# First batch of a gated linear attention: float32 operands on TensorE, keys transposed by TensorE, tap diagonals written by ScalarE

## The chip, the cores and the metric

The kernel runs on one core of one Trainium2 chip. The metric is the device time of one execution in microseconds (us). Engines are named as the profile names them: PE is TensorE (PEld its weight loads), DVE is VectorE, ACT is ScalarE, POOL is GpSimd, SP is SyncE, which here only issues transfers. f16 and f32 are float16 and float32.

## What is computed

Four batches go through three stages. The first is a linear attention with a forget gate per channel; the second a causal convolution of 5 taps that gates a projection; the third a two-dimensional Fourier mix, a normalisation and a two-layer perceptron.

```python
# attention: 4 batches, 8 heads, 768 tokens, 48 channels a head
f = 1.0 / (1.0 + np.exp(-f_logit))
for t in range(S):
    state = f[:, :, t, :, None] * state + np.einsum('bhd,bhe->bhde', k[:, :, t], v[:, :, t])
    y[:, :, t] = np.einsum('bhd,bhde->bhe', q[:, :, t], state)
# gating: 384 channels
gate = sigmoid(causal_conv(x, conv_w))            # 5 taps
x = gate * (x @ w_val) @ w_out
# mix and perceptron
u = x + np.real(fft2(x))
ch = np.maximum(normalised(u) @ w_ch1, 0.0) @ w_ch2
out = u + ch
```

## The kernel before

Everything is float32 at its ends and f16 on TensorE: an operand is split into a high f16 part (written by ACT) and a low f16 part (DVE or POOL subtracts the high one), and a product is three f16 products, high by high, high by low and low by high, added up in PSUM.

A batch of 768 tokens is 6 chunks of 128 (`NC`), and two chunks share one preparation. `Prep` loads the forget logits `f` and the tile `qk` (queries and keys, channels of two heads on 128 partitions, 4 head pairs), forms running sums of log gates on DVE (the scan `f<-sep,f`), their exponentials `e` and `f` on ACT, and multiplies them into `qk` in four steps (`scaled`), each on DVE or POOL by a string of letters: `E0` for the first preparation, `E1` for the others. `Attention.split` makes the f16 parts of a chunk: `qkhl` (ACT high, DVE low), `vz` from the values `v` (ACT high, DVE low), and sends the keys through a transposing DMA into `kt`. `Attention.scores` forms keys by queries, 24 matmuls a chunk into two PSUM tiles; DVE multiplies them by the causal mask into `a`, ACT writes the high part `ah`, POOL the low part `al` of the first half and DVE that of the second (`LO`). `Attention.outputs` forms the chunk's contribution to the state (12 matmuls with `kt`, not in the last chunk), the output `y` (24 matmuls with `vz`), the part from the state so far (12 matmuls with `tb`, not in the first chunk), then updates the state `T` on DVE and splits it into `tb` (ACT high, DVE low). The output goes to `xT` on ACT, partly on through a DMA, and is split again into `xhl`.

In the first batch the convolution is done partly by TensorE: `diagonals` writes 15 taps in two f16 parts as 30 diagonal matrices of 128 by 128 into `fs`, by two POOL instructions, and four of the six gate units multiply `xhl` by them. The tile `fs` is later overwritten by the tables of the Fourier mix. Between the steps of the first batch's attention, other generators are advanced: `small_weights` (`w_out`, `w_val` and the tables made of them) and `mlp_weights`, which decodes the perceptron's weights `w` from 64-bit storage by three DVE steps, a scaling and a high part on ACT and a low part on POOL. 30 matmuls on the constant tile `sep` (`keep_warm(c, PRE)`) stand ahead of the first batch and two more behind each of its first steps; nothing reads their result.

The order of instructions on each engine is set when the program is built, by a scheduler that works from priorities; an instruction's priority is its place in the code, except where `at(c, n)` gives it the fixed place `n`: `LATER` for the perceptron's weights and the second batch's preparations. On the chip each engine runs its list in order.

```python
e.tensor_tensor(parts[:, 1], qk, parts[:, 0], ALU.subtract)          # split: qkhl, low part
nc.sync.dma_start_transpose(out=kt, in_=hl[:, 1].rearrange("p l a w -> p (l a w)"))
for n, (lk, lq) in enumerate(((0, 0), (0, 1), (1, 0))):              # scores: three f16 products
```

Of the kernel before, what the change touches and what calls it, by code (L numbers as in the profile page):

```python
# [22 lines left out]
KT = DM // 128  # L23
# [119 lines left out]
def load_constants(c):  # L143
    nc, T, io = c.nc, c.T, c.io
    c.ident = T([128, 128], F32, "ident")
    nc.sync.dma_start(c.ident, io["ident"])
    c.mask = T([128, CH], F32, "mask")
    nc.sync.dma_start(c.mask, io["mask"])
    c.small = T([128, 5], F32, "small")
    nc.sync.dma_start(c.small, io["small"])  # L150
    c.bmask, c.vs, c.pad, c.bias = c.small[:, 0:2], c.small[:, 2:3], c.small[:, 3:4], c.small[:, 4:5]
    c.ends = T([128, NB, 2, NC, NP], F32, "ends")
    c.pm = T([128, NB, NC, NP, 2], F32, "pm")
    c.xmax = T([128, NB], F32, "xmax")
# [72 lines left out]
def diagonals(c):  # L227
# [9 lines left out]
    nc.gpsimd.tensor_tensor(w[:, 1], w[:, 1], w[:, 0], ALU.subtract)  # L237
    for l in range(2):
        nc.gpsimd.tensor_tensor(c.diagonal[:, l].rearrange("p k t m -> p (k t) m"), c.ident.unsqueeze(1).to_broadcast([128, n, 128]),
                                w[:, l].unsqueeze(2).to_broadcast([128, n, 128]), ALU.mult)  # L240


def small_weights(c):
# [227 lines left out]
class Attention:  # L471
# [19 lines left out]
    def split(self, g):  # L491

        c, nc = self.c, self.c.nc
        b, i = g // NC, g % NC
        qk = self.preps[g // TC].qk[:, :, :, g % TC].rearrange("p a x h w -> p a x (h w)")
        hl = c.T([128, 2, 2, NP, CH], F16, "hl", 2, name="qkhl")
# [7 lines left out]
        self.kt[g] = kt  # L504
        v = self.v.pop(g).rearrange("p (h e) -> p h e", h=NH)
        if i == 0:
            nc.vector.tensor_reduce(c.seen[:, b, 1], v, AX.X, ALU.max, apply_absolute_value=True)
        vz = c.vz[g % 2][:, 0:2 * NH * 2 * HD].rearrange("p (l h w) -> p l h w", l=2, h=NH)[:, :, :, 0:HD]
        nc.scalar.activation(vz[:, 0], v, AF.Copy, scale=c.vs)
        nc.vector.scalar_tensor_tensor(vz[:, 1], v, c.vs, vz[:, 0], ALU.mult, ALU.subtract)  # L510

    def scores(self, g):

        c, nc, hl = self.c, self.c.nc, self.hl[g]
        ps = [c.PS(NP * CH, "p", 4) for _ in range(2)]
# [14 lines left out]
    def outputs(self, g, x):  # L530

        c, nc, mm = self.c, self.c.nc, self.c.mm
        b, i = g // NC, g % NC
        w = 2 * HD
        hl, kt = self.hl.pop(g), self.kt.pop(g).rearrange("p (l a) w -> p l a w", l=2)
# [26 lines left out]
        if i < NC - 1:  # L562
            state = c.state
            pm = c.pm[:, b, i].unsqueeze(3).to_broadcast([128, NP, 2, HD])
            new = ds
            if i:
                nc.vector.tensor_tensor(state, new, state, ALU.add)
                new = state
            nc.vector.tensor_tensor(state, new, pm, ALU.mult)
            parts = c.tb[(i + 1) % 2][:, 0:2 * NP * w].rearrange("p (l w) -> p l w", l=2)  # L570
            flat = state.rearrange("p a h e -> p (a h e)")
# [3 lines left out]
        y4 = y[0:w].rearrange("p (a w) -> p a w", a=NP)  # L575
        at = TAPS - 1 + i * CH
        xf = x.f[0:w, :, at:at + CH]
        nc.scalar.activation(xf[:, :, SUB:], y4[:, :, SUB:], AF.Copy, scale=X_SCALE / OUT_FAR)
        nc.scalar.activation(xf[:, :, SUB - 1::-1], y4[:, :, 0:SUB], AF.Copy, scale=X_SCALE / OUT_NEAR)
        for k in range(KT):  # L580
            nc.sync.dma_start(x.f[w:, k, at:at + CH], x.f[32 * k:32 * k + 32, KT, at:at + CH])
        yield

# [339 lines left out]
def emit(tc, io):  # L923
    c = setup(tc, io)
    with tc.tile_pool(name="sb", bufs=1) as pool, tc.tile_pool(name="ps", bufs=1, space=bass.MemoryType.PSUM) as psum:
# [24 lines left out]
        def others(g):  # L950

            u = g // 2 + 2
            if u < NB * NT:
                if g % 2 == 0:
                    steps[u] = att.preps[u].steps(E1)
                    for _ in range(2):
# [3 lines left out]

        first, second = small, mlp_weights(c, (W1_SCALE, W2_SCALE))
        c.pieces = 0
# [17 lines left out]
        def abc():  # L980
            for b in range(NB):
# [4 lines left out]
                for n, v in enumerate(att.batch(b, x, todo, others)):  # L986
                    if b == 0:
                        aside(first, SIDE[n] if n < len(SIDE) else 1)
                        if n >= WFROM:
                            aside(second, 1, LATER)  # L990
# [19 lines left out]
DEC = 'vvvvvvvvvvvv'  # L1010
E0 = 'vgvg'
E1 = 'gggv'
LO = 'vgv'
# [11 lines left out]
WFROM = 8  # L1025
LATER = 1150
MULTIPLIED = ((0, 0), (0, 1), (0, 2), (1, 0))
# [358 lines left out]
```

## Time and profile before

| | us |
|---|---|
| median of 3 runs | 654.32 |
| lowest and highest run | 653.95, 656.33 |
| the profiled execution | 652.6 |
| its span, first to last instruction | 650.8 |
| mean granted TensorE clock | 0.939 of full speed |

| engine | busy us | share of the span |
|---|---|---|
| PE | 574.1 | 88% |
| DVE | 463.2 | 71% |
| ACT | 292.6 | 45% |
| POOL | 240.6 | 37% |

The shares are means over stages with different limits. The page's row of 40 slices shows this: in the first eight slices (130 us) DVE is at 7 to 9 tenths and PE mostly at 3 to 8, behind them PE is at 9 or more in nearly all. A reading by stage is therefore needed, and the rows for it stand in the section below. Matmul durations in the rows contain the pipeline's depth; what a matmul takes from the engine is the distance between two starts.

### The profile page before, as it was taken

Reading aid. Unit: us, or ns where it says so; the run is one execution under the profiler, and the core shown is the slowest. Engines: PE = TensorE matmul, PEld = TensorE weight load, DVE = VectorE, ACT = ScalarE, POOL = GpSimd, SP = SyncE. Lnnn points to the kernel's source line nnn. Section 1 sums busy time; section 2 is a strip of 40 time slices with the busy share of each in tenths; the row PEclk is TensorE's granted clock in tenths of the full one; section 3 lists DMA queues with packets and bytes.
Section 4 is the critical chain, followed back from the end, with each engine's and each line's share of the span. In section 5 each row is a group of like instructions: output and inputs, shape, how many; then the busy total and the mean of one; then the engine's idle time right before and its main releaser. Section 6 shows DMA issues by size and latency. Waiting matters only on the chain.

```text
span 650.8 us, 12244 instructions
## 1 busy us (share of the span) xinstructions
PE 574.1 (88%) x4920; PEld 409.3 (63%) x4920; DVE 463.2 (71%) x729; ACT 292.6 (45%) x508; POOL 240.6 (37%) x248
## 2 busy tenths in 40 slices
PE   5357865869996899999998999999999999999995
PEld 2135453447675666776677776775677777777773
DVE  5899999787979889346579789265397492463651
ACT  3467687453576664221376644212465532121110
POOL 3778657342457451112348333021362221130000
PEclk9558878789999999999988999999999999999998
DMA  8616775921425560002225440011212000041000
GB/s 310 188 57 202 173 174 148 264 83 49 91 65 168 146 155 32 26 14 61 41 60 175 113 113 25 1 46 29 44 45 66 7 25 1 20 63 41 1 26 30
DMA packets 64435, 54.99 MB, mean 84 GB/s; under 512 B 46416, under 2 KB 55888, under 8 KB 64368
## 3 DMA queue, kind: packets, MB, share of 16 engines
q1 hardware_dynamic: 63824, 52.27, 30.3%
q0 software_dynamic: 544, 1.84, 0.9%
q8 instruction: 40, 0.66, 0.4%
q14 instruction: 27, 0.22, 0.1%
HBM read 37.58 MB, written 4.72 MB: 65 GB/s over the span
## 4 chain that ended last, share of the span: by engine, by line
PE 45%; DVE 26%; DMA 11%; issue 6%; ACT 5%; POOL 4%; SPq 2%; DVEq 0%; POOLq 0%; ACTq 0%
PE c L80 28%; PE p L80 17%; DVE gate L80 6%; DMA qk<-in_qk 4%; DVE w L80 3%; DMA w<-in_w_ch 3%; DVE qkhl L80 2%; SPq L80 2%; DVE eo L80 2%; DMA xT<-xT 2%; DMA f<-in_f 1%; DVE f L80 1%; POOL gd L80 1%; DVE vz L80 1%; DVE hl L80 1%
## 5 line engine op out<-in xcount | busy, mean ns | idle before, releaser
L80 PE MATMUL c<-unT,w 128*128 128x256 f16 x1296 | 193.5, 274 | 0.6 <-DVE unT L80 0.6
L80 PE MATMUL c<-w,hh 128*128 128x384 f16 x576 | 149.7, 327 | 3.3 <-ACT w L80 1.9
L80 PEld LDWEIGHTS <-w 128*128 128x128 f16 x1296 | 126.5, 98 | 23.7 <-issue 0.7
L80 PE MATMUL c<-w,hl 128*128 128x384 f16 x288 | 92.6, 327 | 0.5 <-DVE hl L80 0.5
L80 DVE SCALAR_TENSOR_TENSOR hl<-c,hh 128x512 f16<-128x512 f32 x72 | 49.3, 685 | 60.4 <-ACT hh L80 60.2
L80 ACT ACTIVATE hh<-c 128x512 f16<-128x512 f32 x72 | 42.4, 589 | 94.5 <-PE c L80 92.4
L80 PEld LDWEIGHTS <-hh 128*128 128x128 f16 x576 | 56.1, 98 | 32.9 <-issue 3.7
L80 PE MATMUL p<-qkhl 64*128 64x128 f16 x576 | 54.0, 234 | 22.7 <-DVE qkhl L80 15.3
L80 PEld LDWEIGHTS <-gd 128*128 128x128 f16 x468 | 44.5, 99 | 27.1 <-issue 6.9
L80 PEld LDWEIGHTS <-qkhl 64*128 64x128 f16 x576 | 28.9, 100 | 48.1 <-issue 26.5
L80 PE MATMUL p<-wp,gd 128*128 128x388 f16 x216 | 55.0, 341 | 3.2 <-DVE xc L80 3.2
L80 PE MATMUL p<-ah,vz 128*128 128x128 f16 x384 | 56.2, 233 | 0.0
L80 PEld LDWEIGHTS <-vz 128*128 128x128 f16 x576 | 47.8, 105 | 9.6 <-issue 4.8
L80 POOL TENSOR_TENSOR al<-a,ah 128x512 f16<-128x512 f32 x24 | 37.6, 1566 | 31.0 <-ACT ah L80 31.0
L80 POOL TENSOR_TENSOR xhl<-xT,xhl 128x384 f16<-128x384 f32 x23 | 26.9, 1170 | 54.0 <-ACT xhl L80 54.0
L80 DVE SCALAR_TENSOR_TENSOR gate<-xT,convw,gate 128x768 f32<-128x768 f32 (+1 forms) x44 | 41.5, 996 | 7.1 <-ACT gate L80 7.0
L80 POOL TENSOR_TENSOR rs<-rs,mhalf 128x2 f32<-128x2 f32 x12 | 9.4, 780 | 99.9 <-DVE rs L80 99.9
L80 DVE TENSOR_TENSOR a<-p,mask 128x512 f32<-128x512 f32 x48 | 30.9, 680 | 21.0 <-PE p L80 18.0
L80 PE MATMUL p<-wch,gd 128*128 128x194 f16 x252 | 41.2, 247 | 5.2 <-DVE gd L80 1.8
L80 PE MATMUL p<-al,vz 128*128 128x128 f16 x192 | 41.5, 233 | 3.6 <-DVE al L80 2.4
L80 PE MATMUL p<-xhl,wv 128*128 128x384 f16 x216 | 43.1, 328 | 1.3 <-DVE a L80 0.6
L80 POOL TENSOR_TENSOR qk<-qk,e 128x512 f32<-128x512 f32 x23 | 31.7, 1396 | 32.4 <-ACT e L80 10.1
(149 smaller groups left out, 1068.9 us busy)
## 6 DMA issues: line engine op xcount, KB each, us to landing
qk<-in_qk SPq DMA_DIRECT2D x24, 512.0 KB, 5.4
w<-in_w_ch SPq DMA_DIRECT2D x21, 384.0 KB, 4.4
f<-in_f SPq DMA_DIRECT2D x12, 528.0 KB, 4.2
v<-in_v SPq DMA_DIRECT2D x24, 192.0 KB, 2.8
out_dram<-ot SPq DMA_DIRECT2D x24, 192.0 KB, 1.9
raw<-in_w_out SPq DMA_DIRECT2D x3, 384.0 KB, 4.5
vraw<-in_w_val SPq DMA_DIRECT2D x3, 384.0 KB, 8.0
xT<-xT SPq DMA_DIRECT2D x72, 16.0 KB, 1.8
```

The lines of the kernel that those rows point to most:

```text
L80: r = f(*args, **kw)
```

## The change

For the first batch (`g < NC`) the attention works on float32 operands instead of f16 parts. `whole` takes the place of `split`: four TensorE transposes bring the keys into PSUM, ACT copies them to `ktf`, and ACT scales the values into `vz`, seen as float32. `whole_scores` has 8 float32 matmuls where there were 24 f16 ones, and DVE's masked product `af` is used as it is, without `ah` and `al`. `whole_outputs` has 4, 8 and 4 float32 matmuls where there were 12, 24 and 12; the state is copied to `tb` by one ACT instruction. The other batches go through the code of before (`split_outputs`), and before they use the two `vz` tiles POOL clears them again. `diagonals` becomes a generator: 30 ACT instructions, two to a step, take the place of the two on POOL. The first preparation's four products all go to DVE (`E0`), of the second and third two each (`E1`, one before); the later ones stay as they were (`E2`). `LATER` is 880 where it was 1150.

```diff
-    for l in range(2):
-        nc.gpsimd.tensor_tensor(c.diagonal[:, l].rearrange("p k t m -> p (k t) m"), c.ident.unsqueeze(1).to_broadcast([128, n, 128]),
-                                w[:, l].unsqueeze(2).to_broadcast([128, n, 128]), ALU.mult)
+    for i in range(n):
+        for l in range(2):
+            nc.scalar.activation(c.diagonal[:, l, i // TAPS, i % TAPS], c.ident, AF.Copy, scale=w[:, l, i:i + 1])
+        if i % 2:
+            yield
+    yield
...
+        if b == 0:
+            return self.whole(g, v)
+        if i < 2:
+            nc.gpsimd.memset(c.vz[i].bitcast(U32), 0)
...
+    def whole(self, g, v):
+        c, nc = self.c, self.c.nc
+        qk = self.preps[g // TC].qk[:, :, :, g % TC].rearrange("p a x h w -> p a x (h w)")
+        ps = c.PS(NP * CH, "c1", 2)
+        for p in range(NP):
+            c.tr(ps[:, p * CH:(p + 1) * CH], qk[:, p, 1], c.ident)
+        kt = c.T([128, NP, 128], F32, "kt", 2, name="ktf")
+        nc.scalar.activation(kt.rearrange("p a w -> p (a w)"), ps, AF.Copy)
+        nc.scalar.activation(c.vz[g % 2].bitcast(F32).rearrange("p (h w) -> p h w", h=NH)[:, :, 0:HD], v, AF.Copy, scale=c.vs)
+        self.hl[g], self.kt[g] = qk, kt
+
+    def whole_scores(self, g):
...
+            for p in range(NP):
+                r = slice(64 * hh, 64 * hh + 64)
+                c.mm(ps[:, p * CH:(p + 1) * CH], qk[r, p, 1], qk[r, p, 0], p == 0, p == NP - 1)
+            a = c.T([128, NP, CH], F32, tag, 2, name="af")
+            nc.vector.tensor_tensor(a, ps.rearrange("p (a w) -> p a w", a=NP), c.mask.unsqueeze(1).to_broadcast([128, NP, CH]), ALU.mult)
+            self.a[g].append(a)
+
+    def whole_outputs(self, g):
...
+            for p in range(NP):
+                mm(ds[:, p], kt[:, p], vc[:, p], p == 0, p == NP - 1)
...
+        for p in range(NP):
+            for hh in range(2):
+                mm(y[:, p * CH:(p + 1) * CH], vz[:, (2 * p + hh) * w - HD * hh:][:, 0:128], a[hh][:, p], p == hh == 0,
+                   i == 0 and hh == 1 and p == NP - 1)
...
+                mm(y[:, p * CH:(p + 1) * CH], c.tb[i % 2].bitcast(F32)[:, p * w:][:, 0:128], qk[:, p, 0], False, p == NP - 1)
+        if i < NC - 1:
+            self.new_state(g, ds)
+            nc.scalar.activation(c.tb[(i + 1) % 2].bitcast(F32)[:, 0:NP * w], c.state.rearrange("p a h e -> p (a h e)"), AF.Copy,
+                                 scale=A_SCALE)
...
-E0 = 'vgvg'
-E1 = 'gggv'
+E0 = 'vvvv'
+E1, E2 = 'vgvg', 'gggv'
...
-LATER = 1150
+LATER = 880
```

PE's list at the start of the first batch, before (`sep` is the constant tile of the 30 matmuls ahead, `qkhl` the f16 parts of queries and keys, `raw` a piece of `w_out`):

```order
L80 LDWEIGHTS sep_61
L80 MATMUL c1_186<-sep_61 128x512
L80 LDWEIGHTS qkhl_148
L80 MATMUL p_288<-qkhl_148 128x128
L80 LDWEIGHTS qkhl_148
L80 MATMUL p_289<-qkhl_148 128x128
```

The same place on PE now, with the transposed keys in `c_140` and `c_150`:

```order
L80 MATMUL c_140<-ident,qk 128x128 x4
L80 MATMUL c_150<-ident,qk 128x128 x4
L80 MATMUL p<-qk 128x128 x16
L80 LDWEIGHTS sep
L80 MATMUL c_179<-sep 128x512
```

The 30 matmuls on `sep` stood ahead of all work; now they stand behind the transposes and scores of the first two chunks, and ahead of the first chunk's outputs.

DVE's list behind the first scaling of `qk`, before:

```order
L80 TENSOR_TENSOR qk<-qk,f 128x4x2x64
L80 SCALAR_TENSOR_TENSOR raw<-raw,bits 128x384
L80 TENSOR_SCALAR bits<-raw 128x384
L80 SCALAR_TENSOR_TENSOR bits<-raw,bits 128x384
L80 TENSOR_TENSOR qkhl<-qk,qkhl 128x4x2x128
L80 SCALAR_TENSOR_TENSOR raw<-raw,bits 128x384
L80 TENSOR_TENSOR qkhl<-qk,qkhl 128x4x2x128
L80 TENSOR_TENSOR wpm<-raw 128x192 x2
```

And now, where `af` is the masked scores:

```order
L80 TENSOR_TENSOR qk<-qk,e 128x4x2x64
L80 TENSOR_SCALAR bits<-raw 128x384
L80 TENSOR_TENSOR qk<-qk,f 128x4x2x64 x2
L80 SCALAR_TENSOR_TENSOR bits<-raw,bits 128x384
L80 SCALAR_TENSOR_TENSOR raw<-raw,bits 128x384
L80 TENSOR_SCALAR bits<-raw 128x384
L80 SCALAR_TENSOR_TENSOR bits<-raw,bits 128x384
L80 SCALAR_TENSOR_TENSOR raw<-raw,bits 128x384
L80 TENSOR_SCALAR bits<-raw 128x384
L80 SCALAR_TENSOR_TENSOR bits<-raw,bits 128x384
L80 TENSOR_TENSOR af<-p,mask 128x512
```

Two `qkhl` are gone, two products of `qk` came from POOL, and the first `af` has moved ahead of the third piece's last step.

ACT's list at the same time, before:

```order
L80 ACTIVATE f<-f 128x1056
L80 ACTIVATE qkhl<-qk 128x4x2x128 x2
L80 ACTIVATE raw<-raw 128x384 x2
L80 ACTIVATE vz_91<-v,small 128x8x48
L80 ACTIVATE f<-f 128x1056
L80 ACTIVATE ah<-a 128x512
```

And now, with the diagonals in `fs`:

```order
L80 ACTIVATE f<-f 128x1056
L80 ACTIVATE fs<-ident,cwf 128x128 x20
L80 ACTIVATE ktf<-c_140 128x512
L80 ACTIVATE raw<-raw 128x384
L80 ACTIVATE fs<-ident,cwf 128x128
L80 ACTIVATE ktf<-c_150 128x512
```

Twenty of the 30 diagonals stand ahead of the first copy of transposed keys, on which PE's first matmul on `sep` waits (it reuses the PSUM tile).

## Rows read from the trace of the kernel before

**Rows 1.** Stretches from:to in us: length, busy us per engine (instructions), clock, DMA share, GB/s
```profile
core 0: us, PE busy (x) PEld busy (x) DVE busy (x) ACT busy (x) POOL busy (x), PEclk, DMA share, GB/s
10.00:141.50 131.50, 80.36 (x677) 51.42 (x676) 123.55 (x168) 85.75 (x147) 86.84 (x86) 0.78 0.62 174
```
**Rows 2.** The same view, the two stretches behind it
```profile
141.50:260.00 118.50, 108.11 (x987) 78.69 (x987) 101.60 (x161) 65.75 (x116) 53.03 (x53) 0.96 0.39 100
260.00:645.00 385.00, 377.84 (x3237) 276.14 (x3234) 234.05 (x395) 137.06 (x242) 97.31 (x96) 0.99 0.18 45
```
**Rows 3.** DVE's groups, 10 to 141.5 us: busy us, mean ns | idle ahead, releaser
```profile
L80 DVE TENSOR_TENSOR qkhl<-qk,qkhl 128x1024 f16<-128x1024 f32 x8 | 15.2, 1897 | 3.0 <-ACT qkhl L80 3.0
...
L80 DVE SCALAR_TENSOR_TENSOR vz<-v,small,vz 128x384 f16<-128x384 f32 x8 | 8.2, 1024 | 0.0
L80 DVE TENSOR_TENSOR a<-p,mask 128x512 f32<-128x512 f32 x12 | 7.7, 676 | 0.0
L80 DVE TENSOR_TENSOR qk<-qk,f 128x512 f32<-128x512 f32 x5 | 6.5, 1293 | 0.0
...
L80 DVE TENSOR_TENSOR al<-a,ah 128x512 f16<-128x512 f32 x6 | 5.1, 853 | 0.0
L80 DVE SCALAR_TENSOR_TENSOR raw<-raw,bits 128x384 uint32<-128x384 uint32 x3 | 4.8, 1616 | 0.0
...
L80 DVE SCALAR_TENSOR_TENSOR tb<-T,tb 128x384 f16<-128x384 f32 x5 | 3.4, 672 | 0.0
```
**Rows 4.** POOL's groups in the same stretch
```profile
L80 POOL TENSOR_TENSOR qk<-qk,e 128x512 f32<-128x512 f32 x9 | 12.4, 1394 | 15.3 <-DMA raw<-in_w_out 9.3 <-DMA xT<-xT 4.7 <-ACT e L80 1.3
L80 POOL TENSOR_TENSOR al<-a,ah 128x512 f16<-128x512 f32 x6 | 8.7, 1451 | 3.8 <-ACT ah L80 3.8
L80 POOL TENSOR_TENSOR fs<-ident,cwf 128x1920 f16<-128x1920 f32 x2 | 7.7, 3888 | 0.0
```
**Rows 5.** ACT's groups in the same stretch
```profile
L80 ACT ACTIVATE qkhl<-qk 128x1024 f16<-128x1024 f32 x8 | 8.3, 1048 | 4.9 <-POOL qk L80 4.9
...
L80 ACT ACTIVATE ah<-a 128x512 f16<-128x512 f32 x12 | 7.4, 624 | 2.1 <-DVE a L80 2.0
...
L80 ACT ACTIVATE vz<-v,small 128x384 f16<-128x384 f32 x8 | 4.8, 603 | 0.0
L80 ACT ACTIVATE xT<-p 96x256 f32<-96x256 f32 x12 | 3.9, 364 | 0.0
```
**Rows 6.** PE's groups, 13 to 141.5 us
```profile
L80 PE MATMUL p<-xhl,fs 128*128 128x384 f16 x60 | 13.0, 367 | 10.2 <-ACT xhl L80 10.2
...
L80 PE MATMUL p<-qkhl 64*128 64x128 f16 x144 | 8.4, 261 | 14.5 <-ACT qkhl L80 7.3 <-DVE qkhl L80 7.1
```
**Rows 7.** DVE in order of time: start us, us, what
```profile
12.57 0.68 DVE L80 TENSOR_TENSOR qk<-qk,f 128x512 f32<-128x512 f32 x1
```
**Rows 8.** PE in order of time: start us, us, what, count
```profile
2.21 9.39 PE L80 MATMUL c<-sep 128*128 128x512 f16 x30 [2.21 <-DVE sep L80]
...
22.30 1.36 PE L80 MATMUL p<-qkhl 64*128 64x128 f16 x22 [1.94 <-DVE qkhl L80]
...
38.25 0.31 PE L80 MATMUL p<-al,vz 128*128 128x128 f16 x1
...
38.57 0.31 PE L80 MATMUL p<-al,vz 128*128 128x128 f16 x1
...
49.07 0.22 PE L80 MATMUL p<-al,vz 128*128 128x128 f16 x1
...
49.24 0.22 PE L80 MATMUL p<-al,vz 128*128 128x128 f16 x1
...
49.81 0.79 PE L80 MATMUL p<-qkhl 64*128 64x128 f16 x22
...
158.49 0.82 PE L80 MATMUL c<-ident,un 128*128 128x128 f32 x6
```
**Rows 9.** PE's weight loads in order of time
```profile
158.41 0.66 PEld L80 LDWEIGHTS c<-ident,un 128*128 128x128 f32 x6
```
**Rows 10.** Stretches of PE: length, busy us (instructions), clock, DMA share, GB/s
```profile
7.80:11.60 3.80, 3.80 (x18) 1.00 1.04 373
...
14.60:48.70 34.10, 14.18 (x109) 0.50 0.43 135
```

More of the change, by code (lines that the diff above doesn't have):

```diff
@@ L512, in scores, with new_state @@
+    def new_state(self, g, ds):
+        c, nc = self.c, self.c.nc
+        pm = c.pm[:, g // NC, g % NC].unsqueeze(3).to_broadcast([128, NP, 2, HD])
+        new = ds
+        if g % NC:
+            nc.vector.tensor_tensor(c.state, ds, c.state, ALU.add)
+            new = c.state
+        nc.vector.tensor_tensor(c.state, new, pm, ALU.mult)
     def scores(self, g):
+        if g < NC:
+            return self.whole_scores(g)
         c, nc, hl = self.c, self.c.nc, self.hl[g]
@@ L532, in outputs, with split_outputs @@
         c, nc, mm = self.c, self.c.nc, self.c.mm
-        b, i = g // NC, g % NC
-        w = 2 * HD
+        i, w = g % NC, 2 * HD
+        y = yield from (self.whole_outputs if g < NC else self.split_outputs)(g)
+        y4 = y[0:w].rearrange("p (a w) -> p a w", a=NP)
+        at = TAPS - 1 + i * CH
+        xf = x.f[0:w, :, at:at + CH]
+        nc.scalar.activation(xf[:, :, SUB:], y4[:, :, SUB:], AF.Copy, scale=X_SCALE / OUT_FAR)
+        nc.scalar.activation(xf[:, :, SUB - 1::-1], y4[:, :, 0:SUB], AF.Copy, scale=X_SCALE / OUT_NEAR)
+        for k in range(KT):
+            nc.sync.dma_start(x.f[w:, k, at:at + CH], x.f[32 * k:32 * k + 32, KT, at:at + CH])
+        yield
+    def split_outputs(self, g):
+        c, nc, mm = self.c, self.c.nc, self.c.mm
+        i, w = g % NC, 2 * HD
         hl, kt = self.hl.pop(g), self.kt.pop(g).rearrange("p (l a) w -> p l a w", l=2)
@@ L562, in outputs @@
         if i < NC - 1:
[L563 to L569, printed above, removed]
+            self.new_state(g, ds)
             parts = c.tb[(i + 1) % 2][:, 0:2 * NP * w].rearrange("p (l w) -> p l w", l=2)
-            flat = state.rearrange("p a h e -> p (a h e)")
+            flat = c.state.rearrange("p a h e -> p (a h e)")
             nc.scalar.activation(parts[:, 0], flat, AF.Copy, scale=A_SCALE)
@@ L574, in outputs @@
         yield
[L575 to L582, printed above, removed]
+        return y
     def parts(self, g, x):
@@ L954, in others @@
                 if g % 2 == 0:
-                    steps[u] = att.preps[u].steps(E1)
+                    steps[u] = att.preps[u].steps(E1 if u < NT else E2)
                     for _ in range(2):
@@ L959, in others @@
                     drain(steps[u])
-        first, second = small, mlp_weights(c, (W1_SCALE, W2_SCALE))
+        first, second, third = small, mlp_weights(c, (W1_SCALE, W2_SCALE)), diagonals(c)
         c.pieces = 0
@@ L988, in abc @@
                         aside(first, SIDE[n] if n < len(SIDE) else 1)
+                        aside(third, 1, None, False)
                         if n >= WFROM:
```

27 lines of the change are left out of this document (22 added, 5 removed).

## The prediction

> **What bounds the kernel now.** I read the engines' busy time by stretch first. From 10 to 141.5 us (the first batch's attention and gates, up to the first parts of its Fourier mix, `xc`) DVE is busy for 123.55 of 131.5 us, PE for 80.36, ACT for 85.75, POOL for 86.84 [rows 1]. Behind that PE is the bound: 108.11 of 118.5 us, then 377.84 of 385 [rows 2]. So the first stretch is DVE's, the rest is PE's, and a change in the first stretch is worth what it moves 141.5 us forward.
>
> Next the groups of DVE in that stretch. The reader is to see two things. First, DVE hardly waits: the waits that I find named ahead of these groups are 3.0 us for `qkhl` [rows 3]. Second, durations are uneven: `a`, which reads PSUM, takes 676 ns each time of twelve, while `qk<-qk,f` of the same size from SBUF takes 684 ns once [rows 7] and 1293 ns on average; `qkhl` averages 1897 ns and `raw` 1616 ns [rows 3]. They are long where POOL is at work: POOL's two instructions for the diagonals, 3888 ns each, lie over the longest of them [rows 4]. So DVE loses time to POOL where both its operands lie in SBUF.
>
> Then PE in order of time, for prices. The granted clock is at the lower level (1.2 GHz) from 14.6 to 48.7 us, and PE is busy there for 14.18 of 34.1 us; it had fallen after the 30 matmuls on `sep`, with nothing on PE behind them until the first scores [rows 8, 10].
>
> **The change, part by part.** *DVE.* Six of eight `qkhl` go (two belong to the second batch): at the mean 6 x 1.90 = 11.4 us. Six of eight `vz` go, 6 x 1.02 = 6.1; six `al`, 5.1; five `tb`, 3.4 [rows 3]. Sum 26.0 us. Four products of `qk` come from POOL: between 0.68 and 1.29 us each [rows 3, 7], I take 0.9, since POOL is then less busy: +3.6. Two more pieces of perceptron weights now stand ahead of `xc`, six DVE steps, about as long as the shortest SBUF products: +3.7; these are moved, not added. POOL loses six `al` (8.7), the diagonals (7.8) and four products of `qk` (4 x 1.39 = 5.6): 22 of its 86.84 us, a quarter [rows 1, 4]. The DVE time that POOL costs the remaining instructions I put at 26 us (`qk<-qk,f` alone 5 x (1.29 - 0.68) = 3.0, `raw` about 3, the rest like them), a quarter of which is 6.6. DVE's work up to `xc` becomes 123.6 - 26.0 + 3.6 + 3.7 - 6.6 = 98.3 us. By DVE alone, with its 8 us of waits kept, `xc` would come at 10 + 98.3 + 8 = 116 us, 25 us earlier.
>
> *PE.* Per chunk 24 score products, 24 for `y`, 12 for the state and 12 for `tb` become 8, 8, 4 and 4, and four transposes come in. Over six chunks 144 + 144 + 60 + 60 f16 products go, 48 + 48 + 20 + 20 = 136 f32 products and 24 transposes come. Prices: three f16 products of `y` take 49.24 - 49.07 = 0.17 us at the higher clock and 38.57 - 38.25 = 0.32 at the lower, so 0.056 and 0.107 each; scores, two row halves side by side, 0.79 / 22 = 0.036 and 1.36 / 22 = 0.062 [rows 8]. What goes: 264 x 0.056 + 144 x 0.036 = 20 us at the higher clock, 37 at the lower. An f32 product proper is in no row. Below it is bounded by the f32 transposes, about 0.11 us each (6 weight loads in 0.66 us) [rows 8, 9]; above by four f16 products plus a weight load that nothing hides, 0.22 + 0.14 = 0.36 at the higher clock. I take four f16 products, 0.22 and 0.43: splitting both operands gives four products, and the kernel's own f16 form leaves out the fourth. What comes: 136 x 0.224 + 24 x 0.11 = 33 us at the higher clock, 63 at the lower. The clock was 0.78 on average [rows 1], about half the time at either level: PE gains (33 + 63) / 2 - (20 + 37) / 2 = 19.5 us of work.
>
> The Trainium skill, FP8 and Floating Point Precision, TensorE Precision Notes, says that true FP32 takes four passes through the array, high and low by high and low; that is the upper reading of the two without weight loads, and no trace here shows it. By the transposes' 0.11 us the added work at the higher clock would be 18 us instead of 33 and PE would not come near DVE.
>
> The 30 matmuls on `sep` also move into the stretch. Before, they ran from 2.21 to 11.6 us, when PE had nothing else [rows 8]; now they stand between the first scores and the first outputs. Each is 0.21 us at the higher clock (18 in 3.8 us [rows 10]) or twice that: 6 to 13 us, 1.6 of which already lay behind 10 us, so +8. PE's work in the stretch becomes 80.4 + 19.5 + 8 = 108 us. It can start when DVE has made the last product of the first `qk`: the old one ended at 13.25 [rows 7], two more and their like lie with it, so 13.4. The wait of 10.2 us for the last chunk's `xhl` stays [rows 6], because the way through `xT` and its transfer is untouched. 13.4 + 108 + 10.2 = 131.6: PE allows `xc` at about 131, 10 us earlier. PE, denser, may keep the higher clock longer: all f32 work at it takes 13 us off, while its other waits (14.5 us for `qkhl` [rows 6], which vanish, but waits for `af` and `ktf` come) put some back.
>
> *The start.* Transposes and scores from 13.4: 8 x 0.11 + 16 x 0.22 = 4.4 us at the higher clock, 9 at the lower, then `sep`, then the first chunk's outputs: 26 to 36 us and 3 us for them, where they ended at 38.9 [rows 8]. So the early scores (13.4 for 22.3) pay back 0 to 10 us here.
>
> *ACT.* Six `qkhl` (6.3) and twelve `ah` (7.4) go; six `ktf` come, priced like `ah`, 3.7; the 30 diagonals lie between `xT` (364 ns, 256 columns) and less; with `vz` at 603 ns for 384 I take 0.28, 8.4 us [rows 5]. Net -1.6: nothing. But twenty of them, 5.6 us, stand ahead of the first `ktf`, for which `sep` waits. They need POOL's small weights; if those come at 15 us, `ktf` is there at 21, about when the scores end. Hidden by the scores; without that cover it costs up to 5 us.
>
> *Transfers.* Six transposing DMAs leave the SP queue; DMA share is 0.62 [rows 1] and DVE hardly waited, so I count nothing. POOL's clearing of `vz` for the second batch, two instructions, lies in POOL's idle time. `LATER` moves by as much as the program's instructions in front of it shrink, so the weights stand about where they stood.
>
> **The sum.** DVE allows 25 us, PE 10. The later bound sets it, and the clock's gain and the new waits lie on either side of it; I take 12 us. From `xc` on PE has the same matmuls, and 2 to 3 us of its 10 us of waits up to 260 [rows 2] may go with the two pieces decoded ahead; not counted. 652.6 - 12 = 640.6 for the profiled execution; the median of the runs is 1.7 above it: **642.3 us**.
>
> **The rivals.** *DVE's relief is the whole of it.* If f32 products cost little more than transposes, or the clock stays up, PE drops to about 95 us in the stretch and the gain is 22 to 25: 630 us. For it: PE is denser; against it: no row has such a product. Chance 0.2.
>
> *The start eats it.* Cold scores, `sep` at the lower clock and late diagonals give the early start back, and the gain is 4 to 7 us: 648. Chance 0.1.
>
> *It doesn't do what it says, or is given back.* PE fills the time that DVE frees exactly (the f32 product at 0.31 us: 12 / 136 = 0.09 above 0.224), or the perceptron's weights, whose decoding runs on behind `xc` while DVE is busy for 101.6 of 118.5 us [rows 2], hold the perceptron where it was: 654. Chance 0.1.
>
> *Slower.* An f32 product's weights are not hidden. The f32 weight loads lie at 0.11 us from each other under transposes [rows 9], the product may need them for both halves. At 0.36 us a product PE gets 136 x 0.136 = 18.5 us more, `xc` comes at 148, and the time is 642.3 + 18.5 = 661. It decides from 0.31 us. Against it: loads overlap the matmul in front in the rows of `un`. The Trainium skill, TensorE: Matmul & The Clock Gate, Weight-path perf modes, speaks for it: fast weight load is off when the input is FP32. Chance 0.1.
>
> **How the numbers follow.** The forecast has 0.5, from 637 to 648. A difference of 0.5%, 3.3 us, is about what a measurement can tell from none. Faster by more: 0.5 + 0.2 + 0.1 = 0.8. The same 0.1, slower 0.1. The range leaves out the slower case and the far end of the best one: 628 to 652.
>
> **What would show it.** Right: `xc` at 125 to 133 us, DVE busy about 98 us up to it, `raw` near 0.55 us instead of 1.6, f32 products 0.2 to 0.25 us apart at the higher clock, the first chunk's outputs before 38 us, and the time from `xc` to the end unchanged at 509 us. Wrong: f32 products 0.31 us or more apart, PE waiting for ACT's diagonals, or a tail longer than 509 us.

## The result, and the profile after

The changed kernel takes 661.3 us (median of 4 runs, 660.1 to 662.5) where the kernel before took 654.1 beside it: a ratio of 1.0114, with a 95% interval of 1.0065 to 1.0163. It is slower by about 1.1%. The forecast was 642.3 us, with a range of 628 to 652. The profiled execution took 660.67 us, its span is 658.9 us. Single executions of some kernels below ran slower at a lower granted clock; the times given are medians without them.

The stretches of the trace after, with the columns of [rows 1], cut where the first parts of the Fourier mix, `xc`, now begin:

```profile
core 0: us, PE busy (x) PEld busy (x) DVE busy (x) ACT busy (x) POOL busy (x), PEclk, DMA share, GB/s
10.00:149.10 139.10, 93.53 (x587) 66.79 (x588) 97.85 (x155) 86.57 (x169) 67.91 (x79) 0.84 0.50 160
```

The same moment in the view of one tile (durations in ns, then the start of the first and of the last of three):

```profile
L80 DVE SCALAR_TENSOR_TENSOR xc<-p,xc x3: 552/552/562, 149.1 to 150.1; 128x388 f16<-128x388 f32 x3
```

`xc` starts at 149.1 us instead of 141.5, and from there to the end it takes 658.9 - 149.1 = 509.8 us, where it was 650.8 - 141.5 = 509.3. The whole loss lies ahead of `xc`. The work there is no larger: DVE is busy for 97.85 us, where [rows 1] had 123.55 up to 141.5, and POOL for 67.91 instead of 86.84. Both bounding engines now wait. DVE's and PE's groups of that stretch (busy us, mean ns of one | idle time ahead and its releaser), which answer to [rows 3] and [rows 6]; the last row is of the stretch 10 to 150 us:

```profile
L80 DVE TENSOR_TENSOR af<-p,mask 128x512 f32<-128x512 f32 x12 | 8.0, 682 | 4.7 <-PE p L80 4.6
...
L80 DVE TENSOR_TENSOR qk<-qk,f 128x512 f32<-128x512 f32 x6 | 4.9, 827 | 10.4 <-DMA qk<-in_qk 10.1 <-ACT f L80 0.2
...
L80 DVE TENSOR_TENSOR qk<-qk,e 128x512 f32<-128x512 f32 x4 | 3.0, 739 | 3.6 <-DMA qk<-in_qk 2.3 <-ACT e L80 1.2
...
L80 DVE TENSOR_TENSOR wpm<-raw 128x192 f32<-128x192 f32 x6 | 1.9, 356 | 10.7 <-ACT raw L80 10.7
...
L80 DVE SCALAR_TENSOR_TENSOR raw<-raw,bits 128x384 uint32<-128x384 uint32 x3 | 1.7, 556 | 0.1
...
L80 PE MATMUL p<-xhl,fs 128*128 128x384 f16 x60 | 12.2, 351 | 15.8 <-ACT xhl L80 15.8
```

Two new waits stand out: 10.1 + 2.3 = 12.4 us of DVE for the transfer of `qk`, and 10.7 us for ACT's `raw`. The wait for `xhl` grew from 10.2 [rows 6] to 15.8.

The second of them begins on POOL. Its list in order of time (start us, us, what, in brackets the idle time ahead and its releaser):

```profile
10.47 0.72 POOL L80 COPY ends<-e 128x16 f32<-128x16 f32 x1 [6.46 <-ACT e L80]
21.51 0.19 POOL L80 TENSOR_TENSOR pends<-ends 128x4 f32<-128x4 f32 x1 [10.32 <-issue]
...
22.93 0.22 POOL L80 TENSOR_TENSOR cwf<-cwf 128x15 f32<-128x15 f32 x1
```

Between `ends` and the first product POOL did nothing for 10.32 us, and waited for nothing that the profile shows. In the instruction list a configuration step of POOL stands just there. In the list of before it stood behind the clearings at the start, right ahead of POOL's first product of `qk`. ACT and PE pass the delay on:

```profile
22.88 5.95 ACT L80 ACTIVATE fs<-ident,cwf 128x128 f16<-128x128 f32 x20 [11.00 <-POOL cwf L80]
28.73 0.57 ACT L80 ACTIVATE ktf<-c 128x512 f32<-128x512 f32 x1
29.21 0.54 ACT L80 ACTIVATE raw<-raw 128x384 f32<-128x384 f32 x1
```

```profile
13.35 1.97 PE L80 MATMUL c<-ident,qk 128*128 128x128 f32 x8 [13.35 <-DVE qk L80]
15.24 4.82 PE L80 MATMUL p<-qk 64*128 64x128 f32 x32
29.36 8.54 PE L80 MATMUL c<-sep 128*128 128x512 f16 x30 [9.29 <-ACT ktf L80]
...
40.52 0.83 PE L80 MATMUL p<-af,vz 128*128 128x128 f32 x6
...
51.34 1.98 PE L80 MATMUL p<-af,vz 128*128 128x128 f32 x16
53.15 0.83 PE L80 MATMUL p<-qk,tb 128*128 128x128 f32 x6
```

The first scores come at 13.35 us, but the first chunk's outputs end at 41.35, later than before (38.9 [rows 8]). The last two rows also give the price that no row of before had: a float32 product is two records, and 8 of them (16 records) take 53.15 - 51.34 = 1.81 us, 0.226 each.

The other wait begins on the SP queue, in order of time, first of the kernel before, then of the changed kernel; behind it DVE, ACT and PE:

```profile
28.37 1.05 SPq L80 DMA_DIRECT2D qk<-in_qk  x2
...
65.45 1.04 SPq L80 DMA_DIRECT2D qk<-in_qk  x2
...
111.13 1.79 SPq L80 DMA_DIRECT2D xT<-xT  x3
```

```profile
55.23 0.81 SPq L80 DMA_DIRECT2D qk<-in_qk  x2
...
86.39 0.81 SPq L80 DMA_DIRECT2D qk<-in_qk  x2
...
114.01 1.31 SPq L80 DMA_DIRECT2D qk<-in_qk  x2
116.07 0.33 SPq L80 DMA_DIRECT2D w<-in_w_ch  x1
118.16 3.11 SPq L80 DMA_TRANSPOSE kt<-qkhl  x1
121.35 1.81 SPq L80 DMA_DIRECT2D xT<-xT  x3
```

```profile
93.50 0.69 DVE L80 TENSOR_TENSOR qk<-qk,f 128x512 f32<-128x512 f32 x1 [6.95 <-DMA qk<-in_qk]
```

```profile
113.05 0.64 ACT L80 ACTIVATE xT<-p 96x256 f32<-96x256 f32 x2
...
128.17 0.51 ACT L80 ACTIVATE xhl<-xT 128x384 f16<-128x384 f32 x1
```

```profile
85.30 1.06 PE L80 MATMUL p<-qk,tb 128*128 128x128 f32 x8
...
97.62 3.78 PE L80 MATMUL p<-af,vz 128*128 128x128 f32 x16 [4.22 <-DVE gate L80]
101.20 1.21 PE L80 MATMUL p<-qk,tb 128*128 128x128 f32 x8
...
128.73 0.48 PE L80 MATMUL p<-xhl,fs 128*128 128x384 f16 x1 [15.83 <-ACT xhl L80]
```

`qk` has two buffers. Before, a chunk's `qk` was read for the last time by `split`, two chunks ahead. Now PE reads it up to the chunk's own outputs (`p<-qk,tb`, which end at 86.36), and the next load into that buffer is issued at 86.39. The third and the fourth load of `qk`, issued at 28.37 and 65.45 us before, now go at 55.23 and 86.39. DVE needs the latter at once and stands until 93.5, with all that is queued behind it; PE waits for that in its turn (4.22 us up to 97.62). At the end of the batch ACT has written the last chunk's `xT` by 113.7, but its transfers are issued at 121.35, 7.7 us later (before, 2.3 us): they stand in the SP queue behind a load of `qk`, one of weights and a transpose for the second batch. `xhl` comes at 128.17, and PE stands for 15.83 us.

### The profile page after: what moved, and what is told of

The parts are those of the page before. It is cut to its first block, busy times and chain, and to the rows that moved or that the text cites. A ratio compares the mean times of both kernels' runs of the same rounds, so it can differ in the third digit from the quotient of the medians.

```text
span 658.9 us, 11989 instructions
## 1 busy us (share of the span) xinstructions
PE 578.2 (88%) x4808; PEld 421.0 (64%) x4808; DVE 429.9 (65%) x710; ACT 292.0 (44%) x526; POOL 218.7 (33%) x242
## 4 chain that ended last, share of the span: by engine, by line
PE 53%; DVE 19%; DMA 9%; issue 6%; POOL 5%; ACT 5%; SPq 1%; DVEq 0%; POOLq 0%; ACTq 0%
PE c L80 33%; PE p L80 20%; DMA qk<-in_qk 6%; DVE gate L80 5%; DVE w L80 4%; DMA w<-in_w_ch 2%; DVE eo L80 1%; DMA xT<-xT 1%; POOL w L80 1%; ACT fs L80 1%; SPq L80 1%; DVE T L80 1%; ACT f L80 1%; POOL qk L80 1%; DVE qkhl L80 1%
## 5 line engine op out<-in xcount | busy, mean ns | idle before, releaser
L80 PE MATMUL c<-unT,w 128*128 128x256 f16 x1296 | 195.6, 276 | 1.2 <-DVE unT L80 1.2
L80 ACT ACTIVATE hh<-c 128x512 f16<-128x512 f32 x72 | 42.5, 591 | 98.5 <-PE c L80 94.7
L80 PE MATMUL p<-wp,gd 128*128 128x388 f16 x216 | 52.7, 327 | 2.5 <-DVE xc L80 1.3
L80 PE MATMUL p<-qkhl 64*128 64x128 f16 x432 | 45.0, 227 | 6.8 <-DVE qkhl L80 5.5
L80 PE MATMUL p<-ah,vz 128*128 128x128 f16 x288 | 45.3, 228 | 0.0
L80 PEld LDWEIGHTS <-wv 128*128 128x128 f16 x216 | 21.2, 98 | 32.1 <-issue 19.0
L80 PEld LDWEIGHTS <-hl 128*128 128x128 f16 x288 | 28.0, 98 | 19.9 <-issue 2.5
L80 PEld LDWEIGHTS <-qkhl 64*128 64x128 f16 x432 | 22.4, 96 | 27.9 <-issue 15.2
L80 ACT ACTIVATE f<-f 128x1056 f32<-128x1056 f32 x36 | 38.8, 1077 | 2.9 <-DMA f<-in_f 2.6
L80 PEld LDWEIGHTS <-vz 128*128 128x128 f16 x432 | 37.3, 102 | 3.3 <-issue 0.2
L80 DVE TENSOR_TENSOR a<-p,mask 128x512 f32<-128x512 f32 x36 | 23.2, 682 | 23.3 <-PE p L80 14.4
```

The lines of the kernel that those rows point to most:

```text
L80: r = f(*args, **kw)
```

## The experiments

Theory 1: POOL's step, through the diagonals, holds the start. Theory 2: the longer life of `qk` makes loads late. The rival: float32 products and PE's own work make the stretch as long as it is. Ratios are to the kernel before, run on the same chip; `xc` is the first start in the trace. The changed kernel stands at 1.0114 and 149.1.

**POOL's step early.**

```diff
     nc.gpsimd.memset(c.mhalf, -0.5)
+    first = T([128, 2], F32, "first")
+    nc.gpsimd.tensor_tensor(first, c.mhalf, c.mhalf, ALU.mult)
```

> The changed kernel with one small POOL product added right behind POOL's first clearing, so that POOL's configuration step, which stood between `ends` (10.47 us) and `pends` (21.51), comes at about 2 us. Theory 1 (the 10 us in which POOL gave nothing held the diagonals, the first `ktf` and the matmuls on `sep`): `cwf` is done at about 13 us instead of 23, the first `ktf` ends at 20 instead of 29.3, the first chunk's outputs end at 31 to 33 instead of 41.35, `xc` starts 5 to 10 us before 149.1, the time is 651 to 656. Theory 2 (late loads of `qk` set the stretch): the start comes earlier in the same way, but the loads pay most of it back, `xc` moves by 3 us or less, 658 to 661. Rival (the float32 products and PE's work in the stretch): the start is filled differently, `xc` moves by less than 2 us.

Measured: 655.8 us, 1.0053 (1.0018 to 1.0088), `xc` at 145.5. The gap moved but kept its length, which I had not reckoned with:

```profile
12.47 0.36 POOL L80 TENSOR_TENSOR first<-mhalf 128x2 f32<-128x2 f32 x1 [10.59 <-issue]
```

So `cwf` was done at 17.7 instead of the expected 13, the first `ktf` at 23.9 and the first outputs at 35.7. 5.6 us gained at the start are 3.6 at `xc`; the waits for `qk` stayed (13.0 us on DVE). That is between the two theories.

**A third place for `qk`.** The f16 parts `qkhl` are needed from the second batch on; their memory serves the second preparation.

```diff
-        self.qk = c.T([128, NP, 2, TC, 2, SUB], F32, "qk", 2)
+        if u == 1:
+            self.qk = c.hl.bitcast(F32).rearrange("p (a x c h w) -> p a x c h w", a=NP, x=2, c=TC, h=2)
+        else:
+            self.qk = c.T([128, NP, 2, TC, 2, SUB], F32, "qk", 2)
...
-        hl = c.T([128, 2, 2, NP, CH], F16, "hl", 2, name="qkhl")
+        n = 4 * NP * CH
+        hl = c.hl[:, g % 2 * n:(g % 2 + 1) * n].rearrange("p (x l a w) -> p x l a w", x=2, l=2, a=NP)
```

> The changed kernel with a third place for the tile `qk`: the second preparation's queries and keys lie in the memory that the f16 parts `qkhl` use from the second batch on. Nothing else is edited. Theory 2: DVE's waits for the transfer of `qk` (12.5 us between 10 and 150 us) fall below 3 us, `xc` starts 6 to 10 us before 149.1, the time is 651 to 655. Theory 1: the start is as it was (first outputs end at about 41), `xc` moves by 3 us or less, 658 to 661. Rival (PE's work): the waits for `qk` go and others take their place, `xc` moves by less than 2 us.

Measured: 656.1 us, 1.0047 (1.0017 to 1.0077), `xc` at 141.3. Theory 2's gain of 7.8 us at `xc` (6.7 by the last of the three, 143.4 for 150.1); the time is 1 us above its range. DVE's group in this kernel, 10 to 141.3 us, no longer waits for a transfer:

```profile
L80 DVE TENSOR_TENSOR qk<-qk,f 128x512 f32<-128x512 f32 x5 | 3.6, 740 | 3.0 <-ACT f L80 3.0
```

Where the gain lies is another matter. The end (start plus duration) of the matmuls with `tb`, the last of each chunk's outputs, and the first `xc`, all in us:

| | chunk 1 | 2 | 3 | 4 | 5 | `xc` |
|---|---|---|---|---|---|---|
| kernel before | 52.4 | 67.0 | 80.1 | 95.8 | 103.1 | 141.5 |
| changed kernel | 55.2 | 76.7 | 86.4 | 102.4 | 110.8 | 149.1 |
| place | 56.6 | 77.8 | 88.4 | 103.8 | 110.4 | 141.3 |
| early product and place | 53.1 | 73.9 | 83.0 | 98.5 | 105.1 | 135.2 |
| diagonals behind alone | 51.8 | 76.1 | 86.5 | 102.5 | 110.9 | 148.0 |
| all three | 40.6 | 66.3 | 76.1 | 94.2 | 100.8 | 128.8 |

Up to the last chunk the place gains nothing: DVE's 12.4 us of waits, the largest new number in the groups, did not hold the chunks. The 7.8 us come behind them. The SP queue with the place, where ACT's `xT` ended at 116.1:

```profile
110.45 0.81 SPq L80 DMA_DIRECT2D qk<-in_qk  x2
116.17 1.78 SPq L80 DMA_DIRECT2D xT<-xT  x3
```

Both transposes were issued before 100 us, the last transfers of `xT` go at once, and PE's wait for `xhl` is 5.76 us instead of 15.83.

The first row of the table shows something else. Against the kernel before, the changed kernel is 2.8 us late at chunk 1, 9.7 at chunk 2 and 7.6 at `xc`; from chunk 5 to `xc` the two take the same, 38.4 and 38.3 us. Most of the loss comes in between chunk 1 and chunk 2, 21.5 us instead of 14.6. PE of the changed kernel in that stretch:

```profile
63.28 0.66 PE L80 MATMUL c<-tab,wtl 128*128 128x388 f16 x3
...
64.43 0.66 PE L80 MATMUL c<-ident,qk 128*128 128x128 f32 x4
69.42 1.01 PE L80 MATMUL c<-sep 128*128 128x512 f16 x2 [4.33 <-ACT ktf L80]
```

The transposes of chunk 2's keys stand in PE's list behind the last products for the tables of `w_out` (`tab`), and PE then waits 4.33 us for ACT's `ktf`. Before, chunk 2's outputs (up to 67.0 us) stood ahead of the last of these products (66.79 to 69.6). This way takes 17.5 to 29.1 us in every kernel here with the float32 attention, also with all three repairs, and 14.6 and 14.9 us in the two without it. No run moved the transposes or the tables, so its cause is open.

**Both.**

> The edits of the early POOL product and of the third place for `qk` together. Theories 1 and 2 both true: the gains add up, `xc` starts 13 to 18 us before 149.1, at 131 to 136, and the time is 643 to 648, which is faster than the kernel before (654). Only one true: as that one alone. Rival (the float32 products and PE's work bound the stretch at about 149): 655 or more, with PE busy for nearly all of it.

Measured: 647.5 us, 0.9935 (0.9892 to 0.9978), `xc` at 135.2. The gains add, and a little more: 3.6 + 7.8 against 13.9. The kernel is faster than before (0.65%) with all its float32 products in place, so the rival falls.

**The diagonals back on POOL**, nothing else:

> The changed kernel with the diagonals written by two POOL instructions again, as before the change, at the place where the generator is first advanced; the attention stays float32. Theory 1 (what hurt at the start is that ACT's first `ktf` stands behind diagonals that wait for POOL): `ktf` comes at about 15 us although POOL's gap is where it was, `sep` runs from 15 to 24, the first outputs end at 30 to 35, and `xc` comes 3 to 8 us earlier; POOL's two instructions (3.9 us each) slow DVE again and cost some of it. 654 to 659. Rival (moving the diagonals was worth as much as it seemed, the loss is elsewhere): 661 or more.

Measured: 655.8 us, 1.0073 (1.0038 to 1.0109), `xc` at 143.8. The size is as expected, the way is not: `ktf` came at 15.3, but the first outputs ended at 47.4, because DVE then waited 11.06 us for ACT's `e` while POOL wrote the diagonals (6.75 us from 26.58): that `e` stands in ACT's list behind `wp`, which needs POOL's next instructions.

**The diagonals behind `ktf`**, first with both repairs, then alone. The edit is one argument, with which each step's instructions are held behind the engine's last ones in the code:

```diff
-                        aside(third, 1, None, False)
+                        aside(third, 1)
```

> The kernel with both edits (early POOL product, third place for `qk`; 135.2 us to `xc`, 647.5 us), and the diagonals held behind ACT's instructions of the first two chunks, so that `ktf` stands ahead of all of them in ACT's list. Theory 1 (the diagonals ahead of the first `ktf` still cost the start): `ktf` at 15 us instead of 23, `sep` runs from 15 to 24, ACT's `raw` comes 4 us earlier to DVE, the first chunk's outputs end at 27 to 29 instead of 35, `xc` starts 3 to 6 us before 135.2, 641 to 645. Rival (DVE and the way of the later chunks set `xc`; the start has slack by now): `xc` moves by less than 2 us, 646 to 648.

Measured: 642.4 us, 0.9828 (0.9761 to 0.9894), `xc` at 128.8: 6.4 us earlier than with both repairs alone, a little over the range. `ktf` stands at 14.76; the first outputs end at 31.6, which is later than I had said. This beats both kernels.

> The changed kernel with one edit: the diagonals held behind ACT's instructions of the first two chunks; POOL's configuration step and the place of `qk` are as in the changed kernel. Theory 1 (what POOL's late step cost was the diagonals ahead of `ktf`): `ktf` at 15 us, first outputs at 30 to 33, `xc` at 141 to 146, 653 to 658, as with the early POOL product or better. Rival (POOL's late step held something else as well, `wpm` or `pm`): 659 or more.

> The changed kernel with the diagonals held behind ACT's instructions of the first two chunks, and nothing else, once more for its profile. If the late loads take the start's gain back: the first outputs end at 32 us instead of 41.35, DVE and POOL wait 15 us or more for the transfer of `qk`, and `xc` is within 4 us of 149.1.

Measured, with the diagonals alone moved: 656.9 us, 1.0069 (1.0025 to 1.0114), in the upper part of the expected range; in the second profile the first outputs end at 34.65, 6.7 us earlier than in the changed kernel, and `xc` starts at 148.0, 1.1 us earlier. DVE and POOL wait 13.2 us for `qk` (I had said 15 or more). The gain is lost as expected, but not where: by the table it is 3.4 us at chunk 1 and 0.6 at chunk 2, ahead of the first load for which DVE waits long (issued at 86.52). In both kernels of the table with the diagonals behind, the way from chunk 1 to chunk 2 is longer (24.3 and 25.7 us) than in the three others with the change (20.8 to 21.5); the diagonals, 0.3 us each, are now on ACT's list there. That they are the cause was not tested, and they can't be the whole of it: the run below with the float32 attention, the place and POOL's diagonals has 26.2. With the other two repairs in place the same edit is worth 12.5 us at chunk 1, 7.6 at chunk 2 and 6.4 at `xc`.

**POOL's step late again, with the two other repairs.**

> The changed kernel with the third place for `qk` and the diagonals behind ACT's instructions of the first two chunks; no early POOL product, so that POOL's step stands between `ends` and `pends` as in the changed kernel. Theory (POOL's step costs what waits for the diagonals and nothing else): 640 to 645, as with the early product. Rival (`pm` for the first state and `wpm`, which wait for POOL until 21 to 24 us, hold DVE and PE too): `xc` 3 to 6 us behind 128.8, 645 to 650.

Measured: 650.15 us, 0.9962 (0.9929 to 0.9994), `xc` at 136.4. The rival holds, a little over its range: POOL's step costs 7.6 us at `xc` though no `ktf` waits for a diagonal. ACT's list shows how: `wp` needs what POOL writes into `wpm`, and ACT's second `raw` stands behind it; DVE then waits 8.15 us for that `raw`:

```profile
25.47 0.53 ACT L80 ACTIVATE wp<-wpm 128x388 f16<-128x388 f32 x1 [9.27 <-POOL wpm L80]
25.90 0.52 ACT L80 ACTIVATE raw<-raw 128x384 f32<-128x384 f32 x1
```

```profile
26.45 1.03 DVE L80 TENSOR_TENSOR wpm<-raw 128x192 f32<-128x192 f32 x2 [8.15 <-ACT raw L80]
```

**The 30 matmuls on `sep` ahead again** (with all three repairs; the call stands in front of the first `att.ahead`):

> As the run with the diagonals behind `ktf`, and the 30 matmuls on `sep` ahead of the first transposes again, as before the change. Theory (the 30 matmuls lie on the path between the first scores and the first outputs): they run from 2 to 12 us, the first outputs end at 22 to 25 us, `xc` starts 2 to 6 us earlier than in the run without this edit. Rival (PE falls to the lower clock behind them, as it did before the change, and the products there take twice as long): the start comes earlier, but `xc` moves by less than 2 us or comes later; the granted clock from 15 to 50 us is near 0.5 instead of 0.8.

Measured: 642.8 us, 0.9864 (0.978 to 0.9948), `xc` at 130.5, not earlier than 128.8. The first outputs end at 28.0 instead of 31.6, but the clock is lower, and chunk 1 ends at 45.6 instead of 40.6. The stretch 15 to 50 us, first with the matmuls between the scores and the outputs, then with them ahead:

```profile
15.00:50.00 35.00, 28.80 (x182) 20.15 (x181) 29.83 (x46) 29.54 (x68) 19.34 (x31) 0.94 0.61 216
```

```profile
15.00:50.00 35.00, 26.47 (x147) 21.26 (x146) 24.19 (x41) 27.04 (x64) 19.04 (x39) 0.68 0.58 213
```

**The kernel before with the early product.**

> The kernel before with the early POOL product alone. There the configuration step already stood behind the first clearing and POOL was free again by 13.23 us at the latest, so I expect `xc` within 2 us of 141.5 and no difference in time over 0.4%. If this gains 4 us as in the changed kernel, the early product is worth something for itself and the gain there says nothing on the change.

Measured: 651.95 us, 1.0013 (0.9973 to 1.0053), `xc` at 142.1. No difference, so the early product repairs what the change did.

**The letters of `E0` as before.**

> The changed kernel with the first preparation's letters as before (`E0` is vgvg): two of its four products are POOL's again. With them POOL's first product stands right behind the first clearing, and so does the configuration step. Theory 1 (the letters of `E0` pushed the step behind `ends`, and that held the start): `cwf` at 18 us instead of 23, first outputs end at 32 to 36, `xc` at 143 to 147, 653 to 658, about as with the early POOL product. The loads of `qk` still come late, so not below 650. Rival: the two products cost POOL and the first scores what the step gives: 659 to 662.

Measured: 659.0 us, 1.0119 (1.0072 to 1.0166), `xc` at 145.0. POOL's step is early and the first outputs end at 34.3, as theory 1 says; the time does not follow. The rival's range holds the time: in this kernel `qk<-qk,f` takes DVE 1649 ns on average instead of 827, beside POOL's products. The 4 us at `xc` are less than they look: its three instructions start between 145.0 and 148.8 us there and between 149.1 and 150.1 in the changed kernel, so the last comes only 1.3 us earlier. What spreads them was not taken apart.

**The float32 attention alone**, with diagonals, letters and `LATER` as before, and then with the third place:

> The float32 attention alone: the changed kernel with the diagonals by two POOL instructions, the letters and `LATER` as before. Theory 2 (late loads of `qk` come with the float32 attention itself, since PE reads `qk` up to the outputs): DVE and POOL wait 8 us or more for the transfer of `qk`, `xc` at 141 to 148, 652 to 660, no faster than before. Rival (the edits around it lose the time, the float32 attention gains what I forecast): 640 to 647, `xc` at 128 to 135.

> The float32 attention alone, as the run without the other edits, with the third place for `qk`. Theory 2: the waits for `qk` fall below 2 us, `xc` is 5 to 12 us earlier than in the run without the place, 642 to 649. If it is no faster, the float32 attention is worth nothing without the relief of POOL.

Measured: 651.0 us, 0.9988 (0.9956 to 1.002), `xc` at 141.1; with the place 652.5 us, 1.0031 (0.9997 to 1.0066), `xc` at 138.1. The first time is 1 us under the expected range: float32 alone is worth nothing. The second expectation fell. No wait for `qk` is left there, and it is no faster; of its three `xc` the last starts at 141.2, without the place at 142.1. One row of DVE shows another cause, in both kernels; the first row is of the kernel with the place, the second of the changed kernel:

```profile
20.38 7.16 DVE L80 TENSOR_TENSOR wpm<-raw 128x192 f32<-128x192 f32 x2 [1.74 <-ACT raw L80]
```

```profile
32.40 0.62 DVE L80 TENSOR_TENSOR wpm<-raw 128x192 f32<-128x192 f32 x2
```

The first pair lies under POOL's diagonals. Two further runs part them from the letters.

> The float32 attention with the third place for `qk`, letters and `LATER` as before, and the diagonals by ACT, held behind the instructions of the first two chunks. Theory (POOL's two instructions for the diagonals, 3.4 us each, hold DVE: the pair of `wpm` under them took 7.16 us where others take 0.6): the pair takes 0.6 us, the first outputs end at 32 to 36 instead of 46.5, `xc` at 129 to 135 instead of 138.1, 643 to 648. Rival (the letters carry the gain, POOL's products of `qk` hold DVE): 650 or more, `xc` at 136 or later.

> The float32 attention with the third place for `qk`, the early POOL product and the letters of the change; the diagonals by two POOL instructions, `LATER` as before. Theory (POOL's diagonals hold DVE): a DVE instruction of several us lies beside them again, the first outputs end at 38 to 47, `xc` at 134 to 140, 648 to 654. Rival (the letters carry the gain): 642 to 647.

Measured: with ACT's diagonals 646.1 us, 0.9935 (0.9902 to 0.9968), `xc` at 127.9, the pair at 1.09 us; with the letters instead 653.0 us, 1.0015 (0.9986 to 1.0044), `xc` at 140.2, a pair of 3.82 us and a `raw` of 3.75 behind it. Taking the diagonals off POOL carries the gain, 10.2 us at `xc`; the letters carry none. How the 10.2 us are shared out was not tested: DVE gets back 6 us at that pair, and POOL is free 6.8 us earlier for what stands behind the diagonals, which by itself held ACT and DVE where the diagonals went back to POOL.

**`LATER` as before**, with all three repairs:

> The kernel with the early POOL product, the third place for `qk` and the diagonals behind `ktf` (642.4 us), with `LATER` as before the change (1150 for 880). The prediction held that `LATER` moves by what the program in front of it shrinks and costs nothing: 640 to 645. Rival (two pieces of weights that now stand ahead of `xc` cost DVE 3.7 us there, or pay behind it): `xc` 2 to 4 us earlier and the stretch behind it longer by as much or more, 645 to 650.

Measured: 644.7 us, 0.9896 (0.9846 to 0.9945), `xc` at 127.5. The time is in the first range, and the interval overlaps with that of the run at 880, so the times settle nothing. The traces lean to the rival: 1.3 us earlier at `xc`, but 515.8 us from there to the end against 512.5. Both runs with the float32 attention, 1150 and an `xc` ahead of 130 have such a tail (the other 516.0).

## Why the prediction was wrong, step by step

*The bounds by busy time* held as amounts and failed as a forecast. DVE's work up to `xc` was forecast at 98.3 us and is 97.85. PE's was forecast at 108 and is 93.5, at a higher clock (0.84 for 0.78); how much of the difference the clock makes was not taken apart. (By the prediction's own terms all f32 work at the higher clock takes 48 - 33 = 15 us off, not 13.) But "The later bound sets it, and the clock's gain and the new waits lie on either side of it" left the new waits without a price, and they were the larger part. In the best version DVE has 98.68 us of work up to `xc` at 128.8 (10 to 128.8 us), the same as in the changed kernel, where `xc` comes at 149.1. The 20.3 us between them are waits of DVE, not work.

*"Transfers. ... I count nothing"* is the first step that failed. It looked at how many transfers go, not at when the buffer that each one fills comes free. In the rows of before, `qkhl` is DVE's and ACT's last reading of `qk`; with `qkhl` gone the last reader is PE, two chunks later, and with two buffers the next load waits for it. Price: 7.8 us at `xc`, by the run that takes it away. Not DVE's waits make it up, but SP's list: what the second batch needs comes late and stands ahead of the first batch's last `xT`. "The wait of 10.2 us for the last chunk's `xhl` stays [rows 6], because the way through `xT` and its transfer is untouched" fails with it: the way was untouched, the queue ahead of it was not.

*ACT's diagonals.* "They need POOL's small weights; if those come at 15 us, `ktf` is there at 21" is the second. They came at 23.15. `E0` had made POOL's first product a DVE product, and POOL's configuration step, which stands ahead of its first product, slid from behind the clearings to behind `ends`. The 9.26 us in which POOL stood before, up to its first product at 13.23, were in the trace; they cost nothing there, and I did not ask what ends them. "without that cover it costs up to 5 us" was the right size for the diagonals (6.4 us at `xc`), but POOL's step costs 7.6 us by a second way, through `wpm` and `raw`, which no step mentions.

*The start.* The first scores came at 13.35 us as forecast (13.4). The forecast had the 30 matmuls on `sep` as 8 us of PE's work; put back ahead, they bring nothing at `xc`; the clock is then 0.68 instead of 0.94 in the next 35 us, and the 3.5 us gained at the first outputs are gone by chunk 1. The early scores were to pay back 0 to 10 us; in the changed kernel the first outputs came 2.5 us later than before.

*The way to chunk 2.* The prediction priced the transposes as PE's work, 0.11 us each, and had no term for where they and `ktf` come to stand in the lists of PE and ACT. The table has 6.9 us of loss there against the kernel before. None of the three repairs shortens it by as much as 1 us, and its cause is open.

*The prices.* Float32 products take 0.226 us at the higher clock and 101.20 - 97.62 = 3.58 us for 8, 0.45 each, at the lower; forecast 0.22 and 0.43. Four f16 products at 0.056 [rows 8] make 0.224. The Trainium skill, FP8 and Floating Point Precision, TensorE Precision Notes, says four passes for true FP32; the rows agree. The rival that an f32 product's weights are not hidden (0.36 us) falls, though its 661 us is the measured time: a right time from a wrong mechanism. The diagonals on ACT took 0.3 us each (5.95 for 20), forecast 0.28; `raw` 0.556 us, forecast 0.55.

*POOL's load on DVE* was real, and where the forecast spread it over many instructions it sits in the float32 kernels mostly beside one pair of POOL's, the diagonals. Off POOL they are worth 10.2 us at `xc`, in which DVE's part and POOL's own delay are not separated. The pair of 192-element products under two POOL instructions took 7.16 us instead of 0.62. The Trainium skill, SBUF — State Buffer, Who interferes with whom, says that a DVE instruction with two SBUF inputs contends with a GpSimd instruction that reads SBUF; the row agrees.

*The tail* of 509 us held for the changed kernel (509.8) and is 512.5 for the best one. Whether an earlier `xc` is partly paid back behind it is not settled: the kernels at 880 lie between 508.4 and 513.1, one execution each, and not in the order of their `xc`.

The forecast's time, 642.3 us, and its `xc` at 125 to 133 us are what the kernel does with the three repairs, 642.4 and 128.8. The relief was there; what follows from the change's own edits, among it a longer life of `qk`, a later step of POOL and diagonals ahead of `ktf`, took it and more. That the numbers meet is in part luck. The 12 us were chosen between bounds of 10 and 25, and the sum behind the 10, 13.4 + 108 + 10.2, is made up otherwise in that kernel: 97.18 us of PE's work, 4.1 of wait for `xhl`, and some 14 of waits that have no term.

## What to carry to other kernels

When an edit removes a copy, ask who now reads the original last, and when the next transfer into that buffer can be issued: in a queue that runs in order, a late load holds whatever is listed behind it, and that may be another stage's last transfer. When an edit moves an engine's first instruction of a kind, look at what its idle time at the start had hidden. A sum of busy times bounds a stage from below; where the two largest bounds fall well below the present time, what sets the end is a chain of waits, and repairs of such a chain show their full worth only together (here 3.6, 7.8 and 1.1 us one by one, 20.3 all three).

## What the runs showed of the hardware that was not expected

At POOL's configuration step POOL is idle for 9.8 to 11.4 us and waits for nothing that the profile shows (10.32 in the changed kernel, 10.59, 9.81 and 10.43 with the early product, 11.43 in the run with the place and the diagonals behind). The profile has no instruction for it. In the kernel before the idle time at that step was 9.26 us and put down to a load of `raw`, so there the step took no longer than that. The Trainium skill, GPSIMD Engine Reference, Instruction dispatch, gives about 6 us for the first call of a freshly loaded kernel, without a visible instruction; here the gaps without a releaser are 1.6 to 1.9 times as long.

The 30 matmuls on `sep` between the scores and the outputs, 8 us of PE, cost nothing that their removal to the front gives back: with them there the granted clock is 0.94 from 15 to 50 us, with them ahead 0.68, and `xc` comes no earlier.
